# Sparse attention and a mixer on one core: VectorE with at most one SBUF operand, block sums and second remainders on GpSimd

## The chip, the cores and the metric

The kernel runs on one core of a Trainium2 chip. The core has a matrix engine (TensorE, PE in the profile), a vector engine (VectorE, DVE), an activation engine (ScalarE, ACT), a general engine (GpSimd, POOL) and a queue engine for transfers (SyncE, SP). PE reads SBUF and writes PSUM; DVE and ACT read and write both; POOL works on SBUF alone. The metric is the device time of one execution in microseconds. For the kernel before the change it is 271.68 us (median of three runs, 271.33 to 276.72).

## The reference

q, k and v have the shape 4 x 8 x 768 x 64 (batch, heads, positions, head size), in float32. Attention is sparse: the positions form 12 blocks of 64, and each query sees its own block and the three blocks with the highest gate.

```
k_rep  = k.reshape(B, H, 12, 64, D).mean(axis=3)
gate   = einsum(q, k_rep); blocks after the query's own get -1e9
sel    = the top 3 blocks of each query, and its own block
scores = q @ k.T / 8, only in selected blocks and at or before the query
x      = softmax(scores) @ v, heads side by side: (4, 768, 512)
u      = x + (relu(x^T @ w_tok1) @ w_tok2)^T
out    = u + relu(u @ w_ch1) @ w_ch2
```

A wrong choice of a block changes the output visibly, so the gate is computed to float32 accuracy.

## The kernel before

**Pairs.** The unit of attention is a pair of heads: 16 pairs, four to a batch. For each pair q and k are loaded (L473) and transposed on PE (`transposed`, L420, in float32; k of pairs 8 to 15 in half precision, L513). ACT or DVE evict the transposed q to QT (float32) and k to KA (L302 for ACT, L304 for DVE; both are lines of the helper `copy`). QT is cast to half precision into QA (`q16`, the group QA<-QT). The mask enters the scores as 12 more rows of the contraction: rows 64 to 75 of KA mark the block of a key, those of QA hold 0 for a block that is seen and -1 for others.

**Gate.** For pairs 0 to 7 the block sums of k come from a DVE reduction over the transposed k (L492). For pairs 8 to 15 `block_sums` loads the batch's keys once more (kb, L441) and halves them by additions (L449), copies the result (L453), transposes it (L454) and evicts it (L456). From pair 4 on (THIRDS) the gate is three bfloat16 products: q and the sums are split into a high part and two remainders (R1 at L555, R2 at L557 for q; `thirds_of`, L431 and L433, for the sums). PE forms them (L542 or L564), DVE adds the causal bias and the three parts (gm, L545 or L569), takes the eight largest of 12 (MAX8, L575, ten instructions a pair), compares with the third (ge, L577) and makes the 0 or -1 rows (bn, two instructions, L581). bn then goes to QA by PE transpositions and two evictions (L600, pairs 0 to 7) or by a DVE transpose and four small DMAs on SP (L586, L589, pairs 8 to 15, the set BDMA).

**Scores and mixers.** The scores (L621) go through the exponential on ACT (L628) into E, POOL clears what lies behind the diagonal (L636), PE multiplies with v (L645), and DVE divides (L648, L652). Token mixing is L663, L667, L677 and L680, the transposition of its result L688, L302 and L304. Channel mixing of a batch follows when its four pairs are done: L706 and L712 or L714, then L723 and L726, and the output leaves on SP (L729).

**PSUM.** Scores have two buffers of two banks. Everything else shares four banks (the ring R), of which channel mixing may hold three; at the end it gets the scores' banks too.

**Order.** The program is written out by a planner (`Plan`). Each step has a cost for each engine that may take it and a due time (`pr`): a pair's start, from EARLY and PACE, less a lead from the table L. The planner walks through time, gives each engine the due step that can start, and so fixes the engine of each step and the order on each engine. A step marked `port=True` is kept off the time of any GpSimd step by `shared`: the two take turns on the port. Where PE would be idle before channel mixing begins, filler matmuls on zeros are put in (L768). Steps run in this order on each engine, and waits between engines come from the data.

Of the kernel before, what the change touches and what calls it, by code (L numbers as in the profile page):

```python
# [9 lines left out]
FP = mybir.dt.float32  # L10
# [35 lines left out]
THIRDS = 4  # L46
BDMA = set(range(8, 16))
EARLY, PACE = 5.28, 14.41
L = dict(kd=28.39, qd=27.08, vd=11.34, va=-3.4, kt=12.9, kr=4.36, ke=-7.41, qt=14.51, qe=2.5, q16=14.89, g=13.38,
         b=7.0, k16=18.79, kx=22.66, kc=20.11, r=6.71, kb=28.92, ks=42.68, w1=-1.17, w2=0.38, wc1=18.04, wc2=24.91,  # L50
         tok=9.65, ml=13.72, o0=-3.85, o1=-3.08, o2=0.0, o3=4.03, o4=0.0, o5=2.8, o6=0.0, o7=0.0, o8=4.91, o9=0.0,
         o10=-8.96, o11=0.22, o12=-0.21, o13=-0.53, o14=-3.47, o15=0.77, m0=0.0, m1=0.47, m2=0.0, m3=3.31)
# [207 lines left out]
def kernel(  # L260
# [101 lines left out]
    ks2 = [sb([128, 2, NB], FP, f"ks2_{i}") for i in range(2)]  # L362
    ksr = Ring("ks2", ks2)
# [3 lines left out]
    kspr = Ring("ksp", [ksp])  # L367
    kppr = sring(2, [128, 3, 2, NB], BF, "kpp")
    ks3r = sring(2, [128, 3, NB], FP, "ks3")
# [3 lines left out]
    for t in ks2:  # L373
        nc.gpsimd.memset(t, 0.0)
# [11 lines left out]
    ks32r = sring(1, [128, 3, PPB * 2 * NB], FP, "ks32")  # L386
    ksar = sring(2, [128, NB], FP, "ksa")
    gmr = sring(2, [128, NJ - 1, 2 * NB], FP, "gm")
    m8r = sring(2, [128, NJ - 1, 2, 8], FP, "m8")
    ger = sring(2, [128, NJ - 1, 2 * NB], FP, "ge")  # L390
# [34 lines left out]
    def thirds_of(src, dst, part, rd, kp, pr):  # L425

        def split(e):
            t, o = src.t, ENG[e]
            h = t.bitcast(BF).rearrange("c i (n two) -> c i n two", two=2)[:, :, :, 1]
            for i in range(2):  # L430
                o.tensor_tensor(out=t[:, i + 1], in0=t[:, i], in1=h[:, i], op=ALU.subtract)  # L431
            for x in range(2):
                o.tensor_copy(out=dst(x), in_=part(h, x))  # L433
        P.op({"DVE": (760.0, 840.0), "POOL": (850.0, 930.0)}, split, port=True, rd=rd, wr=[(src, 2), (kp, 0), (kp, 1)], pr=pr)

    def block_sums(b, pr):

        kb, ksn, ks32, t, kp = Buf(kbr), Buf(ksnr), Buf(ks32r), Buf(Rr), Buf(kspr)
        P.op({"POOL": (80.0, 120.0)}, lambda: nc.gpsimd.memset(kb.t[0:1, 0:1], 0.0), wr=[(kb, 0)], pr=pr - L["kb"])
        P.op({"SP": (700.0, 1800.0, 96 * 1100.0 / 16)},  # L440
             lambda: nc.sync.dma_start(out=kb.t, in_=k[b].rearrange("h (n t) d -> (h n) (t d)", t=64)), wr=[(kb, 0)], pr=pr - L["kb"])  # L441
        n = 2048
        while n >= 64:
            step = min(n, 1024)
            for o in range(0, n, step):
                c = {"DVE": (step * 1.1 + 60, step * 1.1 + 140)}
                if n >= 512:
                    c["POOL"] = (step * 2.2 + 60, step * 2.2 + 140)
                P.op(c, lambda e, n=n, o=o, step=step: ENG[e].tensor_tensor(  # L449
                    out=kb.t[:, o:o + step] if n > 64 else ksn.t[:, 0, :], in0=kb.t[:, o:o + step], in1=kb.t[:, n + o:n + o + step], op=ALU.add),  # L450
                    port=True, rd=[(kb, 0)], wr=[(kb, 0)] if n > 64 else [(ksn, 0)], pr=pr - L["ks"])
            n //= 2
        P.op({"DVE": (190.0, 260.0)}, port=True, fn=lambda: nc.vector.tensor_copy(out=ksn.t[:, 1, :], in_=ksn.t[:, 0, :]), rd=[(ksn, 0)], wr=[(ksn, 9)], pr=pr - L["ks"])  # L453
        P.op(pe(slow=1), lambda: nc.tensor.transpose(out=t.t[:, 0:96], in_=ksn.t.rearrange("r g d -> r (g d)"), identity=id32[0:96, 0:96]),  # L454
             rd=[(ksn, 0), (ksn, 9)], wr=[(t, 0)], pr=pr - L["ks"] + 1)
        P.op(dve(96), lambda: nc.vector.tensor_copy(out=ks32.t[:, 0], in_=t.t[:, 0:96]),  # L456
             rd=[(t, 0)], wr=[(ks32, 0)], pr=pr - L["ks"] + 1)
        thirds_of(ks32, lambda x: kp.t[64 * x:64 * x + 64, :, :, x, :],
                  lambda h, x: h.rearrange("r i (q x n) -> r q i x n", q=PPB, x=2)[64 * x:64 * x + 64, :, :, x, :], [(ks32, 0)], kp, pr - L["ks"] + 1)
        return kp  # L460

    def pair(p):
# [4 lines left out]
        early, thirds = p < FIRST, p >= THIRDS  # L467
# [14 lines left out]
        if early:  # L482
            if thirds:
                ks3, kp = Buf(ks3r), Buf(kppr)
                ksa, sums = ks3, lambda i: ks3.t[:, 0, 6 * i:6 * i + 6]
            else:
                ksa, ks2b = Buf(ksar), Buf(ksr)
                sums = lambda i: ksa.t[:, 6 * i:6 * i + 6]
            for i in range(2):
# [3 lines left out]
                    out=sums(i), in_=t.t[:, 0:HS].rearrange("c (n w) -> c n w", w=64), axis=AX.X, op=ALU.add),  # L493
                    rd=[(t, 0)], wr=[(ksa, i)], pr=t0 - L["kr"])
# [4 lines left out]
            if thirds:  # L499
                thirds_of(ks3, lambda x: kp.t[64 * x:64 * x + 64, :, x, :], lambda h, x: h[64 * x:64 * x + 64], [(ks3, 0), (ks3, 1)], kp, t0 - L["kr"] + 0.1)  # L500
            else:
                for x in range(2):
                    P.op({"DVE": (170.0, 220.0)}, port=True, fn=lambda x=x: nc.vector.tensor_copy(out=ks2b.t[64 * x:64 * x + 64, x, :], in_=ksa.t[64 * x:64 * x + 64, :]),
                         rd=[(ksa, 0), (ksa, 1)], wr=[(ks2b, x)], pr=t0 - L["kr"] + 0.1)
# [15 lines left out]

        for i in range(2):
# [15 lines left out]
        gm, m8, ge, bn = Buf(gmr), Buf(m8r), Buf(ger), Buf(bnr)  # L537
# [9 lines left out]
        else:  # L547
            R1, R2 = Buf(R1r), Buf(R2r)
# [3 lines left out]

            def high(t):
                return t.bitcast(BF).rearrange("c (n two) -> c n two", two=2)[:, :, 1]
            P.op({"DVE": (760.0, 840.0), "POOL": (1210.0, 1290.0)}, port=True, fn=lambda e: ENG[e].tensor_tensor(out=R1.t, in0=QT.t[:, 128:S], in1=high(QT.t[:, 128:S]), op=ALU.subtract),  # L555
                 rd=[(QT, 0), (QT, 1)], wr=[(R1, 0)], pr=t0 - L["r"])
            P.op({"DVE": (760.0, 840.0), "POOL": (1210.0, 1290.0)}, port=True, fn=lambda e: ENG[e].tensor_tensor(out=R2.t, in0=R1.t, in1=high(R1.t), op=ALU.subtract),  # L557
                 rd=[(R1, 0)], wr=[(R2, 0)], pr=t0 - L["r"] + 0.1)

            def gate():  # L560
                for j in range(NJ - 1):
                    s = slice(128 * j, 128 * j + 128)
                    for i, a in enumerate([high(QT.t[:, 128:S])[:, s], high(R1.t)[:, s], R2.t[:, s]]):
                        nc.tensor.matmul(out=g.t[:, 3 * W2 * j:3 * W2 * j + 3 * W2], lhsT=a,  # L564
                                         rhs=kpt().rearrange("c i x n -> c (i x n)"), start=(i == 0), stop=(i == 2))
            P.op(pe(*[72] * 15), gate, rd=[(QT, 0), (QT, 1), (R1, 0), (R2, 0), (kp, 0), (kp, 1)], wr=[(g, 0)], pr=t0 - L["g"])
# [4 lines left out]

        def top():
            for j in range(NJ - 1):
                for x in range(2):
                    nc.vector.max(out=m8.t[:, j, x, :], in_=gm.t[:, j, NB * x:NB * x + NB])  # L575
        P.op({"DVE": (730.0, 820.0)}, top, rd=[(gm, 0)], wr=[(m8, 0)], pr=t0 - L["g"] + 0.2)
        P.op({"DVE": (220.0, 300.0)}, port=True, fn=lambda: nc.vector.tensor_tensor(  # L577
            out=ge.t.rearrange("p j (x n) -> p j x n", n=NB), in0=gm.t.rearrange("p j (x n) -> p j x n", n=NB),
            in1=m8.t[:, :, :, 2:3].broadcast_to([128, NJ - 1, 2, NB]), op=ALU.is_ge), rd=[(gm, 0), (m8, 0)], wr=[(ge, 0)], pr=t0 - L["g"] + 0.3)
        for x in range(2):  # L580
            P.op({"DVE": (180.0, 240.0)}, port=True, fn=lambda x=x: nc.vector.scalar_tensor_tensor(  # L581
                out=bn.t[:, 1:, x, 0:NB], in0=ge.t[:, :, NB * x:NB * x + NB], scalar=1.0,
                in1=own[:, :, NB * x:NB * x + NB], op0=ALU.subtract, op1=ALU.max), rd=[(ge, 0), (fixed, "cst")], wr=[(bn, x)], pr=t0 - L["g"] + 0.4)
        if p in BDMA:
            bnt = Buf(bntr)
            P.op({"DVE": (520.0, 600.0)}, lambda: nc.vector.transpose(  # L586
                out=bnt.t.rearrange("p j x n -> p (j x n)"), in_=bn.t.rearrange("p j x n -> p (j x n)")), rd=[(bn, 0), (bn, 1)], wr=[(bnt, 0)], pr=t0 - L["b"])
# [6 lines left out]
        else:  # L594
# [6 lines left out]
            P.op(pe(*[128] * 5), btr, rd=[(bn, 0), (bn, 1)], wr=[(bt, 0)], pr=t0 - L["b"])  # L601
# [210 lines left out]
```

## Time and profile before

| | before |
|---|---|
| median of the runs | 271.68 us |
| the profiled execution | 271.58 us |
| its span, first to last instruction | 269.9 us |
| PE busy | 254.8 us (94%) |
| DVE busy | 180.6 us (67%) |
| ACT busy | 161.0 us (60%) |
| POOL busy | 116.1 us (43%) |
| granted clock | 0.999 |

A row of a group names a line, an engine, an operation and tiles (output<-input), then its count, busy time, the mean of one in ns, and the idle time of the engine ahead of it with what ended it. Ends of matmuls are modelled, so PE's busy time overlaps a little. 1.7 us of the execution's time lie outside the span.

### The profile page before, as it was taken

How to read it: one execution, taken by the hardware profiler on the slowest of the kernel's cores; microseconds unless marked ns; L12 is line 12 of the kernel's file. 1: busy time of each engine (PE TensorE's matmuls, PEld its weight loads, DVE VectorE, ACT ScalarE, POOL GpSimd, SP SyncE). 2: the span in 40 equal slices, each digit the busy share in tenths (PEclk: the TensorE clock that was granted, in tenths of full speed). 3: DMA queues.
4: the chain of work that ended last, by engine and by line, in shares of the span. 5: the costliest groups of instructions: out<-in, count | busy, mean ns of one | idle time of the engine just before them, and what ended most of it. 6: DMA issues, size and time to landing. Idle time of an engine off the chain costs nothing.

```text
span 269.9 us, 6806 instructions
## 1 busy us (share of the span) xinstructions
PE 254.8 (94%) x2634; PEld 174.9 (65%) x2634; DVE 180.6 (67%) x545; ACT 161.0 (60%) x259; POOL 116.1 (43%) x194
## 2 busy tenths in 40 slices
PE   7799999989999998979999899999999999999993
PEld 7677877766676665736777466767666665554541
DVE  5899999997697688897788565859657532301102
ACT  2679989846674684448983467466675471260520
POOL 7137866885364855573685343445152020000000
PEclk9999999999999999999999999999999999999999
DMA  8999989979907999514999740111001200212103
GB/s 169 222 216 197 234 187 227 233 186 192 188 3 198 217 230 238 123 39 116 178 175 221 177 115 5 41 44 41 5 4 43 83 2 0 78 41 78 39 0 118
DMA packets 87088, 33.10 MB, mean 123 GB/s; under 512 B 80592, under 2 KB 83280, under 8 KB 86864
## 3 DMA queue, kind: packets, MB, share of 16 engines
q1 hardware_dynamic: 82112, 28.22, 47.6%
q0 software_dynamic: 3232, 3.93, 8.5%
q10 hardware_dynamic: 1712, 0.52, 1.0%
q8 instruction: 20, 0.33, 0.5%
q14 instruction: 12, 0.10, 0.1%
HBM read 30.01 MB, written 6.29 MB: 135 GB/s over the span
## 4 chain that ended last, share of the span: by engine, by line
PE 74%; DVE 13%; ACT 5%; issue 3%; DMA 3%; SPq 1%; POOL 1%; DVEq 0%
PE pm L706 17%; PE pm L723 14%; PE sc L621 11%; PE pm L645 6%; PE sc L723 5%; PE pm L420 4%; ACT E L628 3%; PE pm L677 3%; PE pm L663 3%; PE sc L706 3%; PE pm L564 2%; DVE bn L581 2%; DMA k<-in_k_dram 2%; DVE QA L304 2%; DVE u L680 2%
## 5 line engine op out<-in xcount | busy, mean ns | idle before, releaser
L628 ACT ACTIVATE E<-sc 128x1024 f16<-128x1024 f32 (+1 forms) x96 | 84.0, 920 | 16.2 <-PE sc L621 15.2
L636 POOL TENSOR_SCALAR_AFFINE_SELECT E<-E 128x256 f16<-128x256 f16 x96 | 41.1, 435 | 73.5 <-ACT E L628 72.7
L706 PE MATMUL pm<-uT,wc 128*128 128x384 f16 x340 | 64.8, 326 | 1.9 <-DVE os L726 1.9
L723 PE MATMUL pm<-wc,h 128*128 128x512 f16 x228 | 59.5, 379 | 0.0
L706 PEld LDWEIGHTS <-wc 128*128 128x128 f16 x384 | 36.3, 98 | 26.1 <-issue 2.6
L621 PE MATMUL sc<-QA,KA 76*128 76x512 f16 (+3 forms) x256 | 49.2, 305 | 1.5 <-DMA QA<-bnt 1.1
L712 ACT ACTIVATE h<-pm 128x384 f16<-128x384 f32 x60 | 29.6, 493 | 24.0 <-PE pm L706 23.8
L723 PEld LDWEIGHTS <-h 128*128 128x128 f16 x288 | 26.8, 98 | 23.0 <-issue 1.0
L621 PEld LDWEIGHTS <-KA 76*128 76x128 f16 x256 | 22.9, 98 | 16.5 <-DMA QA<-bnt 1.5
L645 PEld LDWEIGHTS <-E 128*128 128x128 f16 x672 | 24.9, 98 | 3.9 <-POOL ks L431 0.8
L645 PE MATMUL pm<-VA,E 128*128 128x65 f16 x651 | 25.6, 193 | 0.5 <-POOL ks L431 0.5
L304 DVE CAST QA<-QT 64x768 f16<-64x768 f32 x22 | 17.9, 812 | 5.9 <-ACT QT L302 5.5
L726 DVE TENSOR_TENSOR os<-u,sc 128x512 f32<-128x512 f16 x5 | 3.3, 687 | 26.0 <-PE sc L723 26.0
L726 DVE TENSOR_TENSOR os<-u,pm 128x512 f32<-128x512 f16 x19 | 12.9, 681 | 11.1 <-PE pm L723 9.6
L714 DVE TENSOR_SCALAR h<-pm 128x384 f16<-128x384 f32 x25 | 13.7, 554 | 8.5 <-PE pm L706 8.0
L479 POOL CAST VA<-v 128x768 f16<-128x768 f32 x16 | 13.3, 837 | 12.6 <-DMA v<-in_v_dram 9.3
L652 DVE TENSOR_TENSOR x<-pm,rc 128x384 f16<-128x384 f32 x31 | 17.2, 554 | 0.8
L302 ACT COPY QT<-pm 128x384 f32<-128x384 f32 x26 | 11.9, 484 | 9.0 <-PE pm L420 8.3
L680 DVE TENSOR_TENSOR u<-x,pm 128x384 f16<-128x384 f16 x30 | 15.5, 548 | 2.5 <-PE pm L677 2.4
L723 PE MATMUL sc<-wc,h 128*128 128x512 f16 x60 | 15.1, 379 | 0.3 <-DVE x L652 0.3
L420 PE MATMUL pm<-id,q 128*128 128x128 f32 x96 | 14.5, 275 | 0.0
L557 POOL TENSOR_TENSOR R<-R 128x640 bf16<-128x640 f32 x10 | 13.4, 1344 | 1.9 <-DVE R L555 1.6
(93 smaller groups left out, 369.2 us busy)
## 6 DMA issues: line engine op xcount, KB each, us to landing
k<-in_k_dram SPq DMA_DIRECT2D x32, 192.0 KB
v<-in_v_dram SPq DMA_DIRECT2D x16, 384.0 KB
out_dram<-os SPq DMA_DIRECT2D x24, 256.0 KB
q<-in_q_dram SPq DMA_DIRECT2D x30, 192.0 KB
wc<-in_moe_w_ch_dram POOLq DMA_DIRECT2D x8, 384.0 KB, 7.5
kb<-in_k_dram SPq DMA_DIRECT2D x2, 1536.0 KB
w<-in_moe_w_tok_dram POOLq DMA_DIRECT2D x2, 384.0 KB, 7.2
QA<-bnt SPq DMA_DIRECT2D x32, 9.0 KB
```

Of the source, the lines that this page charges most:

```text
L304: e.tensor_copy(out=out, in_=in_)
L420: nc.tensor.transpose(out=t[:, 128 * j:128 * j + 128], in_=src.t[:, 3 * i + j].rearrange("p x d -> p (x d)"), identity=id32)
L621: nc.tensor.matmul(out=s.t[:, at:at + 128 * m], lhsT=KA.t[:, x, 128 * kk:128 * kk + 128], rhs=QA.t[:, q0:q0 + m, x, :], start=True, stop=True)
L628: nc.scalar.activation(out=E.t[:, 1024 * g_:1024 * g_ + WIDTH[g_]], in_=s.t[:, 0:WIDTH[g_]], func=AF.Exp, scale=scale)
L636: nc.gpsimd.affine_select(out=o, in_=o, pattern=[[0, 2], [1, 128]], compare_op=ALU.is_ge, fill=0.0, base=0, channel_multiplier=-1)
L645: nc.tensor.matmul(out=t[:, jq, :], lhsT=E.t[:, cc:cc + 128], rhs=VA.t[:, x, kk, :], start=(kk == 0), stop=(kk == jq))
L652: P.op(dve(384), lambda a=a, rc=rc, x=x: nc.vector.tensor_tensor(out=xp.t[:, :, 64 * x:64 * x + 64], in0=a.t[:, 0:NJ * 65].rearrange("p (j ...
L680: P.op(dve(128 * n), lambda m=m, j0=j0, n=n: nc.vector.tensor_tensor(out=u.t[:, c, j0:j0 + n, :], in0=xp.t[:, j0:j0 + n, :], in1=m.t[:, 0: ...
L706: nc.tensor.matmul(out=m.t[:, 0:HS], lhsT=wc1[:, c, 128 * f:128 * f + 128], rhs=uT.t[:, c, HS * i:HS * i + HS], start=(c == 0), stop=(c == ...
L712: nc.scalar.activation(out=h2.t[:, f, :], in_=m.t[:, 0:HS], func=AF.Relu)
L723: nc.tensor.matmul(out=m.t, lhsT=h2.t[:, f, 128 * jj:128 * jj + 128], rhs=wc2[:, f, :], start=(f == 0), stop=(f == NFC - 1))
L726: P.op(dve(DM), lambda j=j, m=m, o=o: nc.vector.tensor_tensor(out=o.t.rearrange("p (c d) -> p c d", d=128), in0=u.t[:, :, j, :], in1=m.t.r ...
```

## The change

The comparison writes 0 or 1 for "below the third largest" into the gate's PSUM bank, MAX8 writes there too, and the bias step is one product of that with `own`. The remainder R1 is taken from the transposed q in PSUM, half by half; R2 is GpSimd's alone. The reduction of pairs 0 to 3 writes to PSUM, and a product with a mask of ones (`side`) replaces the two copies. Block sums in steps of at most 512 columns, their copy and the splits are GpSimd's. The casts of q may go to ACT too. Pairs 4 to 7 use the DMA path for bn. The leads and start offsets in L have other values, and with them the planner's order is another one throughout: the kernel has 67 filler matmuls in place of 100, DVE takes 11 casts of q in place of 22, GpSimd 6 in place of 10 and ACT 15 in place of none.

```diff
-THIRDS = 4
-BDMA = set(range(8, 16))
-EARLY, PACE = 5.28, 14.41
+EARLY, PACE = 5.1, 13.21
...
+         m3=1.67, th=4, bd=4)
...
+    side = sb([128, 2, 6], FP, "side")
+    nc.gpsimd.memset(side, 0.0)
+    for x in range(2):
+        nc.gpsimd.memset(side[64 * x:64 * x + 64, x], 1.0)
...
-        P.op({"DVE": (760.0, 840.0), "POOL": (850.0, 930.0)}, split, port=True, rd=rd, wr=[(src, 2), (kp, 0), (kp, 1)], pr=pr)
+        P.op({"POOL": (850.0, 930.0)}, steps, rd=rd, wr=[(src, 2), (kp, 0), (kp, 1)], pr=pr)
...
-            step = min(n, 1024)
+            step = min(n, 512)
             for o in range(0, n, step):
-                c = {"DVE": (step * 1.1 + 60, step * 1.1 + 140)}
-                if n >= 512:
-                    c["POOL"] = (step * 2.2 + 60, step * 2.2 + 140)
-                P.op(c, lambda e, n=n, o=o, step=step: ENG[e].tensor_tensor(
+                P.op({"POOL": (step * 2.15 + 60, step * 2.15 + 140)}, lambda n=n, o=o, step=step: nc.gpsimd.tensor_tensor(
...
+                if not thirds:
+                    P.op({"DVE": (150.0, 220.0)}, lambda t=t, i=i: nc.vector.tensor_tensor(
+                        out=ks2b.t[:, :, 6 * i:6 * i + 6], in0=t.t[:, HS:HS + 6].rearrange("c (o n) -> c o n", o=1).broadcast_to([128, 2, 6]),
+                        in1=side, op=ALU.mult), rd=[(t, 1)], wr=[(ks2b, i)], pr=t0 - L["kr"] + 0.1)
...
+            if thirds:
+                a, z = (128, HS) if i == 0 else (HS, S)
+                P.op(dve(z - a), lambda t=t, i=i, a=a, z=z: nc.vector.tensor_tensor(
+                    out=R1.t[:, a - 128:z - 128], in0=t.t[:, a - HS * i:z - HS * i], in1=upper(QT.t[:, a:z]), op=ALU.subtract),
+                    rd=[(t, 0), (QT, i)], wr=[(R1, i)], pr=t0 - L["r"])
...
-            P.op({"POOL": (800.0, 860.0), "DVE": (500.0, 580.0)}, q16, port=True, rd=[(QT, 0), (QT, 1)], wr=[(QA, (x, 0))], pr=t0 - L["q16"])
+            P.op({"POOL": (800.0, 860.0), "DVE": (500.0, 580.0), "ACT": (680.0, 780.0)}, q16, port=True, rd=[(QT, 0), (QT, 1)], wr=[(QA, (x, 0))], pr=t0 - L["q16"])
...
+            P.op({"POOL": (1210.0, 1290.0)}, lambda: nc.gpsimd.tensor_tensor(out=R2.t, in0=R1.t, in1=upper(R1.t), op=ALU.subtract),
+                 rd=[(R1, 0), (R1, 1)], wr=[(R2, 0)], pr=t0 - L["r"] + 0.1)
...
+        m8 = lambda: g.t[:, 384:464].rearrange("p (j x n) -> p j x n", x=2, n=8)
+        below = lambda: g.t[:, 0:W2 * (NJ - 1)].rearrange("p (j x n) -> p j x n", x=2, n=NB)
...
-        P.op({"DVE": (220.0, 300.0)}, port=True, fn=lambda: nc.vector.tensor_tensor(
-            out=ge.t.rearrange("p j (x n) -> p j x n", n=NB), in0=gm.t.rearrange("p j (x n) -> p j x n", n=NB),
-            in1=m8.t[:, :, :, 2:3].broadcast_to([128, NJ - 1, 2, NB]), op=ALU.is_ge), rd=[(gm, 0), (m8, 0)], wr=[(ge, 0)], pr=t0 - L["g"] + 0.3)
-        for x in range(2):
-            P.op({"DVE": (180.0, 240.0)}, port=True, fn=lambda x=x: nc.vector.scalar_tensor_tensor(
-                out=bn.t[:, 1:, x, 0:NB], in0=ge.t[:, :, NB * x:NB * x + NB], scalar=1.0,
-                in1=own[:, :, NB * x:NB * x + NB], op0=ALU.subtract, op1=ALU.max), rd=[(ge, 0), (fixed, "cst")], wr=[(bn, x)], pr=t0 - L["g"] + 0.4)
-        if p in BDMA:
+        P.op({"DVE": (220.0, 300.0)}, lambda: nc.vector.tensor_tensor(
+            out=below(), in0=gm.t.rearrange("p j (x n) -> p j x n", n=NB), in1=m8()[:, :, :, 2:3].broadcast_to([128, NJ - 1, 2, NB]), op=ALU.is_lt),
+            rd=[(gm, 0), (g, 1)], wr=[(g, 0)], pr=t0 - L["g"] + 0.3)
+        P.op({"DVE": (220.0, 300.0)}, lambda: nc.vector.tensor_tensor(
+            out=bn.t[:, 1:, :, 0:NB], in0=below(), in1=own.rearrange("p j (x n) -> p j x n", n=NB), op=ALU.mult),
+            rd=[(g, 0), (fixed, "cst")], wr=[(bn, 0)], pr=t0 - L["g"] + 0.4)
+        if p >= L["bd"]:
```

More of the change, by code (lines that the diff above doesn't have):

```diff
@@ L423, in halves, with upper, split, steps @@
         return slice(HS * i, HS * i + HS)
-    def thirds_of(src, dst, part, rd, kp, pr):
-        def split(e):
-            t, o = src.t, ENG[e]
+    def upper(t):
+        return t.bitcast(BF).rearrange("c (n two) -> c n two", two=2)[:, :, 1]
+    def split(src, dst, part, rd, kp, pr):
+        def steps():
+            t, h = src.t, [upper(src.t[:, i]) for i in range(3)]
+            for i in range(2):
+                nc.gpsimd.tensor_tensor(out=t[:, i + 1], in0=t[:, i], in1=h[i], op=ALU.subtract)
             h = t.bitcast(BF).rearrange("c i (n two) -> c i n two", two=2)[:, :, :, 1]
-            for i in range(2):
-                o.tensor_tensor(out=t[:, i + 1], in0=t[:, i], in1=h[:, i], op=ALU.subtract)
             for x in range(2):
-                o.tensor_copy(out=dst(x), in_=part(h, x))
-        P.op({"DVE": (760.0, 840.0), "POOL": (850.0, 930.0)}, split, port=True, rd=rd, wr=[(src, 2), (kp, 0), (kp, 1)], pr=pr)
+                nc.gpsimd.tensor_copy(out=dst(x), in_=part(h, x))
+        P.op({"POOL": (850.0, 930.0)}, steps, rd=rd, wr=[(src, 2), (kp, 0), (kp, 1)], pr=pr)
     def block_sums(b, pr):
@@ L466, in pair @@
         t0 = T(p) + L[f"o{p}"]
-        early, thirds = p < FIRST, p >= THIRDS
+        early, thirds = p < FIRST, p >= L["th"]
         q32, k32, v32 = Buf(q32r), Buf(k32r), Buf(v32r)
@@ L482, in pair @@
         if early:
[L483 to L488, printed above, removed]
+            ks2b = kp = Buf(kppr if thirds else ksr)
+            ks3 = Buf(ks3r) if thirds else None
             for i in range(2):
@@ L499, in pair @@
             if thirds:
-                thirds_of(ks3, lambda x: kp.t[64 * x:64 * x + 64, :, x, :], lambda h, x: h[64 * x:64 * x + 64], [(ks3, 0), (ks3, 1)], kp, t0 - L["kr"] + 0.1)
-            else:
-                for x in range(2):
-                    P.op({"DVE": (170.0, 220.0)}, port=True, fn=lambda x=x: nc.vector.tensor_copy(out=ks2b.t[64 * x:64 * x + 64, x, :], in_=ksa.t[64 * x:64 * x + 64, :]),
-                         rd=[(ksa, 0), (ksa, 1)], wr=[(ks2b, x)], pr=t0 - L["kr"] + 0.1)
+                split(ks3, lambda x: kp.t[64 * x:64 * x + 64, :, x, :], lambda h, x: h[64 * x:64 * x + 64], [(ks3, 0), (ks3, 1)], kp, t0 - L["kr"] + 0.1)
         else:
```

55 lines of the change are left out of this document (21 added, 34 removed).

## The prediction

> **What bounds the kernel now.** I read the slices of the page first, to see which engine is full in which stage.
>
> ```profile
> PE   7799999989999998979999899999999999999993
> ...
> DVE  5899999997697688897788565859657532301102
> ...
> DMA  8999989979907999514999740111001200212103
> ```
>
> PE is full nearly everywhere, VectorE (DVE) and the DMA engines only in the first eight or nine slices of 6.75 us. I cut the span at the first real transposition (6.24 us), at the first channel matmul (L706, 56.96 us) and where the last matmuls are issued (264.16 us). The view by windows gives busy time (and count) of PE, PE's weight loads, DVE, ACT and POOL, then clock, DMA share and GB/s:
>
> ```profile
> 6.24:56.96 50.72, 47.33 (x648) 39.56 (x649) 47.86 (x166) 41.35 (x63) 31.28 (x60) 1.00 1.11 209
> 56.96:264.16 207.20, 201.41 (x1938) 130.32 (x1936) 128.50 (x370) 118.15 (x194) 79.91 (x115) 1.00 0.44 100
> ```
>
> The first of these stretches (call it early) is paced by DVE: 47.86 of 50.72 us busy, with ACT at 41.35, and PE padded with filler matmuls on zeros. The second (late) belongs to PE: 201.41 of 207.20 us, so 5.79 us idle is all that a faster DVE or GpSimd (POOL) can return there. The clock is full (1.00), so it is no term. The chain of waits names most of those 5.79 us (total us, times, longest); PE's rows:
>
> ```profile
> PE pm L706 <- DVE os L726: 1.9, 1, 1.9
> ...
> PE sc L621 <- DMA QA<-bnt: 1.1, 1, 1.1
> ...
> PE pm L564 <- DVE ksp L433: 0.9, 1, 0.9
> ...
> PE pm L600 <- DVE bn L581: 0.8, 1, 0.8
> ```
>
> The largest, 1.9 us, shows what the change is about. The timelines of DVE, POOL and PE there (start, length, instruction):
>
> ```profile
> 116.64 3.48 DVE L581 SCALAR_TENSOR_TENSOR bn<-ge,cst 128x60 f16<-128x60 f32 x2
> ```
>
> ```profile
> 114.40 1.81 POOL L555 TENSOR_TENSOR R<-QT 128x640 f32<-128x640 f32 x1 [1.68 <-ACT QT L302]
> 116.29 1.45 POOL L557 TENSOR_TENSOR R<-R 128x640 bf16<-128x640 f32 x1
> 117.70 2.34 POOL L449 TENSOR_TENSOR kb<-kb 96x1024 f32<-96x1024 f32 x1
> ```
>
> ```profile
> 120.76 0.81 PE L706 MATMUL pm<-uT,wc 128*128 128x384 f16 x4 [1.93 <-DVE os L726]
> ```
>
> Two tiny bias steps last 3.48 us and end (120.12) just as POOL's 2.34 us addition ends (120.04). The eviction queued behind them (os) is late, and PE stands. By tile (min/median/max ns) this is a pattern:
>
> ```profile
> L581 DVE SCALAR_TENSOR_TENSOR bn<-ge,cst x32: 206/218/2378, 14.0 to 207.6; 128x60 f16<-128x60 f32 x32
> L304 DVE CAST QA<-QT x22: 533/554/1517, 9.4 to 200.2; 64x768 f16<-64x768 f32 x22
> L577 DVE TENSOR_TENSOR ge<-gm,m x16: 270/280/579, 13.4 to 206.9; 128x120 f32<-128x120 f32 x16
> L569 DVE TENSOR_TENSOR gm<-pm,cst x12: 276/283/283, 39.4 to 205.1; 128x120 f32<-128x120 f32 x12
> ```
>
> DVE instructions with both operands in SBUF, or copying SBUF to SBUF, stretch to 2 to 11 times their median; those with one operand in PSUM (gm) never do: 276 to 283 ns.
>
> **The change part by part.** Prices are from these groups by form (count, busy us, mean ns):
>
> ```profile
> L636 POOL TENSOR_SCALAR_AFFINE_SELECT E<-E 128x256 f16<-128x256 f16 x96 | 41.1, 435 | 73.5 <-ACT E L628 72.7
> ...
> L304 DVE CAST QA<-QT 64x768 f16<-64x768 f32 x22 | 17.9, 812 | 5.9 <-ACT QT L302 5.5
> L652 DVE TENSOR_TENSOR x<-pm,rc 128x384 f16<-128x384 f32 x31 | 17.2, 554 | 0.8
> ...
> L557 POOL TENSOR_TENSOR R<-R 128x640 bf16<-128x640 f32 x10 | 13.4, 1344 | 1.9 <-DVE R L555 1.6
> ...
> L479 POOL CAST VA<-v 128x768 f16<-128x768 f32 x16 | 13.3, 837 | 12.6 <-DMA v<-in_v_dram 9.3 <-PE pm L645 2.7 <-PE pm L663 0.5
> ...
> L575 DVE MAX8 m<-gm 128x8 f32<-128x12 f32 x160 | 13.2, 158 | 0.3
> ...
> L581 DVE SCALAR_TENSOR_TENSOR bn<-ge,cst 128x60 f16<-128x60 f32 x32 | 10.6, 368 | 0.2
> ...
> L302 ACT COPY KA<-pm 64x768 f16<-64x768 f16 x10 | 7.9, 794 | 1.6 <-PE pm L513 1.5
> ...
> L449 POOL TENSOR_TENSOR kb<-kb 96x1024 f32<-96x1024 f32 x3 | 7.0, 2344 | 0.0
> ...
> L586 DVE STREAM_TRANSPOSE bnt<-bn 128x384 f16<-128x384 f16 x8 | 4.6, 573 | 0.1
> ...
> L449 DVE TENSOR_TENSOR kb<-kb 96x1024 f32<-96x1024 f32 x3 | 4.3, 1420 | 0.0
> ...
> L555 DVE TENSOR_TENSOR R<-QT 128x640 f32<-128x640 f32 x5 | 4.2, 848 | 0.0
> ...
> L600 PE MATMUL pm<-id,bn 128*64 128x128 f16 x40 | 3.7, 224 | 0.8 <-DVE bn L581 0.8
> ...
> L668 DVE TENSOR_SCALAR h<-pm 128x256 f16<-128x256 f32 x4 | 1.7, 418 | 0.8 <-PE pm L663 0.8
> ...
> L449 POOL TENSOR_TENSOR kb<-kb 96x512 f32<-96x512 f32 x1 | 1.3, 1267 | 0.0
> ...
> L431 POOL TENSOR_TENSOR ks<-ks 128x96 f32<-128x96 f32 x2 | 0.7, 348 | 0.1
> ```
>
> *Costs the trace does not show.* The comparison and the bias step now read PSUM: nearest are 0.283 (gm) and 0.418 (128x256), taken 0.283, since the size is gm's. The bias step's two halves (10.6/32 = 0.33 each) become one, so a pair saves 0.66 - 0.28 = 0.38 us of DVE. MAX8 into PSUM: 0.083 each as now (13.2/160), or 0.158 if PSUM writes do not overlap, 0.075 x 10 = 0.75 us a pair; taken 0.083, as it reads the same data; 0 to 12 us of DVE over 16 pairs stays in the range. The remainder R1 becomes 0.418 + 0.554 = 0.97 us on DVE in place of 0.85 there or a GpSimd step. The 64x768 cast of q that ACT may now take: 0.794 from PSUM, and 0.418 to 1.0 as outer ends; taken 0.794.
>
> The Trainium skill ("VectorE: DVE Perf Modes", section on the TRN2 errata) speaks against moving operands: it gives VectorE 58 cycles plus length from SBUF but 120 from PSUM, by estimate 62/0.96 = 65 ns more for each of 64 instructions (24 R1, 16 comparisons, 16 bias steps, 8 block masks), 4.1 us of DVE in all. This trace disagrees: 280 ns (ge, both in SBUF) against 283 (gm, one in PSUM), 0.2 us in all.
>
> *Early stretch.* The program's own order of instructions (read from the built program, engine by engine) holds in the changed kernel, up to the first channel matmul, the same 30 exponentials and 30 masks, but one pair's gating more. ACT gets six casts of q, 6 x 0.794 = +4.8 us (its other differences cancel): 41.35 + 4.8 = 46.1 of 50.72. DVE: two casts less -1.1; bias steps 10 x 0.33 against 6 x 0.28, -1.6; one maximum, comparison and final addition more, 0.83 + 0.28 + 0.28 = +1.4; two transposes +1.1; six R1 pieces against two whole steps 2.9 - 1.7 = +1.2; one split of four small steps less, -1.1 at 0.28; eight block masks for eight copies, at most +0.9; three q evictions more, one reduction less (+1.1 at 0.554) and four smaller evictions less (-1.7 at 0.418). Sum about +0.2. Casts blocked by GpSimd cost 0.812 on the mean against a median of 0.554, so the five of this stretch lose up to 1.3 us that may go. DVE thus stays at 46.8 to 48.1, ACT rises to 46.1: from one pacing engine to two. GpSimd keeps its 31 of 50.72 (two casts of q less, one R2 more). I take 0.5 us won, bounds -2.9 (all DVE idle, 50.72 - 47.86, squeezed out) to +4.8 (every added ACT cast lands on the path).
>
> *Late stretch.* Distances on PE are counted in matmuls between two places of the program's order, each group at its spacing in the chain, as the channel groups with 0.65 us:
>
> ```profile
> 64.31 0.65 PE pm L706 x4
> ```
>
> Pairs 4 to 7 also leave PE's bias transposition: 20 of 40 matmuls, 3.7/2 = 1.85 us, three quarters of it here: 1.4. The idle waits: 1.9 goes (the bias steps have PSUM operands, and the second remainder and sums beside them block nothing); 0.8 goes (the transposition waited for belongs to pair 5, which takes the DMA path); 1.1 goes, because the order puts pair 11's gate 18.9 us of matmuls ahead of its scores, against 12.5 now. Together 3.8, leaving 5.79 - 3.8 = 2.0.
>
> What comes: the block sums, on GpSimd alone. For batch 2 they are seven additions of 512, 7 x 1.267 = 8.9, and by the slope between 512 and 1024 (2.1 ns a column, 0.19 fixed) 0.73 + 0.46 + 0.33 for the short ones, a copy by the same 0.3: 10.7 us. Between the first of them and the split the order sets six masks 2.6, one R2 1.3, three casts 2.5, the split itself 1.4 (4 x 0.35): 18.5 us of GpSimd. PE has 17.7 us of matmuls from there to pair 8's gate (L564), plus some 0.5 for the transposition and its copy. So that gate is about 1.3 us late with no mask waiting; this takes the place of the 0.9 that stood there. Batch 3's sums end 12 us of matmuls ahead of their gate and cost nothing. For waits that a new order brings elsewhere I allow half of what is left, 1.0. Late idle: 2.0 - 0.9 + 1.3 + 1.0 = 3.4 in place of 5.79. DVE itself has room here (128.50 of 207.20 us), so the R1 pieces it gains and the sums it loses cost and bring nothing beyond the waits named.
>
> *SP's queue.* Pairs 4 to 7 add 16 small DMAs, four in a row. The queue's own timeline, and a landing in the chain:
>
> ```profile
> 163.18 3.31 SPq L589 DMA_DIRECT2D QA<-bnt  x4
> ```
>
> ```profile
> 48.44 8.13 SPq L441 DMA_DIRECT2D kb<-in_k_dram  x1
> ```
>
> ```profile
> 152.83 2.00 DMA QA<-bnt
> ```
>
> Each group holds SP 3.3 us, and until it is ready the loads of q and v behind it wait, in a stretch where DMA share is above 1 and one load needed 8.13 us to issue. It is covered as long as gate and scores of these pairs stand apart: 12.6, 15.5, 13.2 and 10.4 us of matmuls in the changed order (7.3, 5.4, 7.8, 7.7 now), against some 3 us of DVE, 3.3 of issue and 2 of landing. Without that cover each pair costs up to 5 us.
>
> *PSUM banks.* The gate's bank is now held through maximum, comparison and bias step, 0.83 + 0.28 + 0.28 = 1.4 us longer a pair, and q's two banks until the R1 pieces are done, up to 0.97. Transpositions, gates, attention outputs and the mixers share four banks, so PE may stand for a free one. No row of before names such a wait. Late, channel matmuls on other banks keep PE fed; early I bound it by 0 and four pairs at 1.4, 5.6 us, and take nothing, because the early order also puts gates of pairs 4 and 5 some 5 to 10 us further ahead of their scores than before. That end, 272.9, lies within the range.
>
> *Sum.* 56.96 - 0.5 = 56.5; late 201.41 - 1.4 + 3.4 = 203.4; tail as before, 269.9 - 264.16 = 5.74: a span of 265.6 us. The profiled execution took 271.58 us with a span of 269.9, so 1.7 lies outside, and it is 0.1 below the median 271.68. Predicted: 267.3 us.
>
> **The rivals.**
>
> *The full gain.* Late idle nearly vanishes (below 0.5) and early DVE loses all its idle: 54.1 + 200.5 + 5.74 + 1.7 = 262. For: every named wait involves a blocked DVE. Against: DMA and ACT are close behind.
>
> *ACT takes over early.* Half of the added casts land on the path, +2.4: 59.4 + 203.4 + 5.74 + 1.7 = 270.2. For: ACT reaches 91% of the stretch. Against: 9.4 us idle now.
>
> *The blocking stays.* If GpSimd also held instructions with one SBUF operand, the 3.8 would stay: 271.1. Against: gm never stretches.
>
> *Slower: GpSimd becomes the bound at batch 2's sums.*
>
> ```profile
> POOL E L636 <- ACT E L628: 72.7, 57, 7.8
> ```
>
> Its masks are queued between the additions and it waits for exponentials: 72.7/57 = 1.3 us a time now. If all six waits fall into that chain, the gate is 1.3 + 7.6 = 8.9 us late: 267.3 + 7.6 = 274.9. It decides from 4.4 us beyond my 1.3. For: no spare time in that chain. Against: when PE stands, its exponentials are long done, so waits shrink. The Trainium skill ("GPSIMD Engine Reference", section on engine selection) advises VectorE for two-input elementwise work, GpSimd being about twice as slow; the trace agrees less strongly, 2344 against 1420 ns for 1024 columns.
>
> **How the numbers follow.** Forecast (265 to 269.5) 0.45, full gain (261.5 to 265) 0.22, ACT or blocking (269.5 to 272.5) 0.20, slower (up to 279) 0.13. Two per cent, about what a measurement of this kernel can tell from no change, is 266.2 below and 277.1 above. Faster beyond it: the full gain and a quarter of the forecast, 0.34; slower beyond it: the upper part of the last case, 0.09; within: 0.57. The range leaves out the far halves of the outer cases: 262.5 to 273.5.
>
> **What would show it.** Right: the bias step at one length near 0.28 us; no PE wait for os; late PE idle near 3.4 us; PE waiting for ksp about 1 us; first channel matmul near 56.5 us. Wrong: ACT near 95% before it and its start beyond 58 us; MAX8 groups above 1.2 us; PE waiting for ksp or QA<-bnt several us; stretched DVE steps with a PSUM operand.

## The result, and the profile after

The changed kernel takes 284.04 us (median of four runs, 282.82 to 285.27) where the kernel before took 271.59 beside it (271.33 to 276.72): a ratio of 1.046, 95% interval 1.039 to 1.053. One execution of the kernel before, the one of 276.72 us, ran in a slower state and is not in the ratio. The changed kernel is slower, and the 267.3 us predicted lie far off. The profiled execution took 282.82 us with a span of 281.1.

The same two stretches in the view by windows, cut at the first real transposition (6.31 us), the first channel matmul (68.06) and the issue of the last matmuls (275.40); columns as before:

```profile
6.31:68.06 61.75, 51.98 (x616) 42.19 (x617) 51.90 (x171) 45.67 (x69) 29.95 (x63) 0.89 0.90 157
68.06:275.40 207.34, 199.29 (x1915) 128.87 (x1913) 115.06 (x335) 120.60 (x195) 79.79 (x137) 1.00 0.48 105
```

The early stretch is 11.0 us longer (61.75 against 50.72). The late one is as long as before, though PE has 2.1 us less to do: its idle time is 8.05 us where 3.4 was forecast. The clock is 0.89 in the first. The page's busy times, its slices and its chain of waits, by line:

```profile
PE 257.8 (92%) x2581; PEld 176.3 (63%) x2581; DVE 171.7 (61%) x516; ACT 167.8 (60%) x265; POOL 115.1 (41%) x216
...
PE   7579798989998999888999999899898999999994
...
DVE  5785799999777563898575676837758351301002
...
PEclk9996689999999999999999999999999999999998
```

```profile
PE pm L702 16%; PE pm L719 13%; PE sc L617 10%; DVE pm L572 9%; PE sc L719 5%; PE pm L641 5%; PE pm L418 5%; DMA k<-in_k_dram 3%; PE sc L702 3%; DVE gm L563 3%; PE pm L673 3%; PE pm L659 2%; DVE x L648 2%; PE pm L684 2%; PE pm L542 1%
```

L572 is MAX8, and its 9% are by far the largest entry of any engine but PE. Its group, then one pair's ten in the timeline, in the changed kernel:

```profile
L572 DVE MAX8 pm<-gm 128x8 f32<-128x12 f32 x160 | 29.1, 182 | 5.3
```

```profile
10.85 2.13 DVE L572 MAX8 pm<-gm 128x8 f32<-128x12 f32 x10
```

and the same ten in the kernel before:

```profile
12.31 0.82 DVE L575 MAX8 m<-gm 128x8 f32<-128x12 f32 x10
```

Ten take 2.13 us in place of 0.82. From one start to the next, (0.82 - 0.157) / 9 = 0.074 us became (2.13 - 0.18) / 9 = 0.216, which is longer than the instruction itself (0.182). That is 1.31 us a pair, 20.9 us of VectorE over 16 pairs. PE's waits in the late stretch of the changed kernel (total us, times, longest), all of 0.8 us or more:

```profile
PE pm L702 <- DVE bn L577: 1.2, 1, 1.2
PE pm L507 <- DVE R L525: 1.1, 1, 1.1
PE pm L702 <- DVE x L648: 1.1, 1, 1.1
PE pm L673 <- DVE x L648: 0.9, 1, 0.9
PE pm L719 <- DVE bn L577: 0.9, 1, 0.9
PE pm L673 <- DVE os L722: 0.8, 1, 0.8
PE pm L641 <- DVE bn L577: 0.8, 1, 0.8
```

The first of them in the timelines of DVE and PE:

```profile
129.68 2.13 DVE L572 MAX8 pm<-gm 128x8 f32<-128x12 f32 x10
131.85 0.29 DVE L574 TENSOR_TENSOR pm<-gm,pm 128x120 f32<-128x120 f32 x1
132.17 0.28 DVE L577 TENSOR_TENSOR bn<-pm,cst 128x120 f16<-128x120 f32 x1
```

```profile
132.50 1.46 PE L702 MATMUL pm<-uT,wc 128*128 128x384 f16 x8 [1.21 <-DVE bn L577]
```

A channel matmul does not read bn. It waits for the gate's bank, which it is to write and which the bias step is the last to read: the maxima delay that step by 1.3 us, and PE waits 1.21.

Of PE's four longest pauses in the early stretch three lie behind maxima too. Two of them are shown here, the first with the ACT step that it goes back to. VectorE's maxima ran from 10.85 to 12.98 us, and its reductions (L486) behind them until 13.90. The next maxima ran from 17.47 to 19.60, ahead of a block mask (L490):

```profile
14.31 0.52 PE L418 MATMUL pm<-id,q 128*128 128x128 f32 x3 [2.21 <-ACT QT L301]
```

```profile
13.47 0.47 ACT L301 CAST KA<-pm 64x384 f16<-64x384 f32 x1 [1.67 <-DVE pm L486]
```

```profile
20.37 0.90 PE L418 MATMUL pm<-id,k 128*128 128x128 f32 x3 [1.21 <-DVE ks L490]
```

Why the ten became slow is seen in the built program, not in the profile. This is what each instruction on VectorE waits for, before the change and after it:

```
before   Max m8<-gm 128x8       [waits DVE]
         Max m8<-gm 128x8  x9
after    Max pm<-gm 128x8  x10  [waits DVE]
```

With the maxima in SBUF the first waits for gm, and nine follow freely. With the maxima in PSUM each one waits for VectorE's own semaphore (the counter by which an engine tells that an instruction has ended), that is for the end of the one before it. The program orders the ten writes to one bank, though they go to different columns; ten writes to different columns of one SBUF tile it leaves free.

### The profile page after: what moved, and what is told of

The parts are those of the page before. It is cut to its first block, busy times and chain, and to the rows that moved or that the text cites. A ratio compares the mean times of both kernels' runs of the same rounds, so it can differ in the third digit from the quotient of the medians.

```text
span 281.1 us, 6723 instructions
## 1 busy us (share of the span) xinstructions
PE 257.8 (92%) x2581; PEld 176.3 (63%) x2581; DVE 171.7 (61%) x516; ACT 167.8 (60%) x265; POOL 115.1 (41%) x216
## 4 chain that ended last, share of the span: by engine, by line
PE 68%; DVE 21%; issue 4%; DMA 3%; ACT 1%; POOL 1%; SPq 0%; DVEq 0%
PE pm L702 16%; PE pm L719 13%; PE sc L617 10%; DVE pm L572 9%; PE sc L719 5%; PE pm L641 5%; PE pm L418 5%; DMA k<-in_k_dram 3%; PE sc L702 3%; DVE gm L563 3%; PE pm L673 3%; PE pm L659 2%; DVE x L648 2%; PE pm L684 2%; PE pm L542 1%
## 5 line engine op out<-in xcount | busy, mean ns | idle before, releaser
L632 POOL TENSOR_SCALAR_AFFINE_SELECT E<-E 128x256 f16<-128x256 f16 x96 | 38.6, 409 | 80.4 <-ACT E L624 80.0
L702 PE MATMUL pm<-uT,wc 128*128 128x384 f16 x332 | 62.3, 326 | 2.4 <-DVE bn L577 1.2
L719 PE MATMUL pm<-wc,h 128*128 128x512 f16 x216 | 56.3, 379 | 1.2 <-DVE bn L577 0.9
L708 ACT ACTIVATE h<-pm 128x384 f16<-128x384 f32 x64 | 31.4, 491 | 23.5 <-PE pm L702 22.1
L572 DVE MAX8 pm<-gm 128x8 f32<-128x12 f32 x160 | 29.1, 182 | 5.3
L448 POOL TENSOR_TENSOR kb<-kb 96x512 f32<-96x512 f32 (+2 forms) x18 | 19.9, 1115 | 1.0 <-DMA kb<-in_k_dram 1.0
L551 POOL TENSOR_TENSOR R<-R 128x640 bf16<-128x640 f32 x12 | 15.0, 1252 | 10.9 <-DVE R L525 10.7
L525 DVE TENSOR_TENSOR R<-pm,QT 128x256 f32<-128x256 f32 (+1 forms) x24 | 11.3, 486 | 10.6 <-ACT QT L301 10.5
L673 PE MATMUL pm<-h,w 128*128 128x128 f16 x186 | 14.2, 219 | 3.5 <-DVE h L664 1.0
L719 PE MATMUL sc<-wc,h 128*128 128x512 f16 x72 | 16.6, 379 | 0.0
```

The lines of the kernel that those rows point to most:

```text
L448: P.op({"POOL": (step * 2.15 + 60, step * 2.15 + 140)}, lambda n=n, o=o, step=step: nc.gpsimd.tensor_tensor(out=kb.t[:, o:o + step] if n > ...
L572: nc.vector.max(out=m8()[:, j, x, :], in_=gm.t[:, j, NB * x:NB * x + NB])
L632: nc.gpsimd.affine_select(out=o, in_=o, pattern=[[0, 2], [1, 128]], compare_op=ALU.is_ge, fill=0.0, base=0, channel_multiplier=-1)
L673: nc.tensor.matmul(out=m.t[:, 128 * j:128 * j + 128], lhsT=w2[:, t, 128 * (j0 + j):128 * (j0 + j) + 128], rhs=h1.t[:, t, :], start=(t == 0 ...
L702: nc.tensor.matmul(out=m.t[:, 0:HS], lhsT=wc1[:, c, 128 * f:128 * f + 128], rhs=uT.t[:, c, HS * i:HS * i + HS], start=(c == 0), stop=(c == ...
L708: nc.scalar.activation(out=h2.t[:, f, :], in_=m.t[:, 0:HS], func=AF.Relu)
```

## The experiments

In the three groups of runs the kernel before itself took anything from 270.2 to 280.7 us, so the kernels below are compared with one another, and only the last paragraph of this section compares with it.

**The thresholds back in SBUF**, with every engine's order left as in the changed kernel:

```diff
+    m8s = [sb([128, NJ - 1, 2, 8], FP, f"m8_{i}") for i in range(2)]
-        m8 = lambda: g.t[:, 384:464].rearrange("p (j x n) -> p j x n", x=2, n=8)
+        m8 = lambda: m8s[p % 2]
```

> The changed kernel with one edit: the ten MAX8 of a pair write their thresholds into an SBUF tile, as before the change; the comparison reads them there. The order of every engine is that of the changed kernel. Theory A (a MAX8 into PSUM starts 0.216 us after the last one in place of 0.075, and these 1.3 us a pair hold up the gates of the early pairs, so that TensorE idles and its clock is lowered): a group of ten takes about 0.8 us again, the first channel matmul comes near 57 us in place of 68.06, the granted clock stays above 0.95 early, and the time is 268 to 274 us. Theory B (the loss lies in the other edits and in the new order: the casts of q on ScalarE, the block sums and second remainders on GpSimd, the other leads): the groups take 0.8 us too, but the first channel matmul stays beyond 65 us and the time above 280 us.

Measured: 267.6 us (265.97 to 269.56). The group, the two stretches, and all of PE's listed waits in the late one:

```profile
L573 DVE MAX8 m<-gm 128x8 f32<-128x12 f32 x160 | 13.1, 157 | 0.3
```

```profile
6.20:59.12 52.92, 47.95 (x616) 39.37 (x617) 46.69 (x171) 45.44 (x69) 29.82 (x63) 0.97 1.06 183
59.12:258.94 199.82, 198.42 (x1916) 129.28 (x1914) 106.53 (x335) 120.11 (x195) 80.19 (x137) 1.00 0.50 109
```

```profile
PE pm L642 <- POOL E L633: 1.1, 2, 0.7
```

The whole loss hangs on where the maxima go, with every other edit in place. The early stretch is 8.8 us shorter than in the changed kernel, the late one 7.5; the waits for bn, R and x are gone. Theory B falls. The first channel matmul came at 59.12, not quite at the 57 expected, and the clock did not stay up throughout: its mean early is 0.97, but it was at half from about 27 to 30.5 us.

**The same change in the kernel before**, and its twin with the bank kept as long but the maxima in SBUF (the last line; in both kernels the planner lays out the steps anew, and the two orders are the same):

```diff
-        gm, m8, ge, bn = Buf(gmr), Buf(m8r), Buf(ger), Buf(bnr)
+        gm, ge, bn = Buf(gmr), Buf(ger), Buf(bnr)
+        m8 = lambda: g.t[:, 384:464].rearrange("p (j x n) -> p j x n", x=2, n=8)
...
+        m8 = lambda: m8s[p % 2]
```

> The kernel before with one edit: the ten MAX8 of a pair write into columns 384 to 463 of the bank that holds the pair's gate, and the comparison reads them there; the bank is kept until then, and the planner lays the steps out anew with that. Theory A: a group of ten takes about 2.1 us in place of 0.8, and the time is 6 to 16 us above that of its twin, in which the bank is kept as long but the thresholds are in SBUF, with a lower granted clock early. Theory B: within 2 us of the twin.

> The twin: the kernel before, with the bank of a pair's gate kept until the comparison is done, as if the thresholds were in it, but with the thresholds in SBUF; the planner's order is that of the run with the thresholds in PSUM. It tells what the longer hold of the bank and the new order cost by themselves. Theory A: within 3 us of the kernel before (268 to 275 us). Theory A2 (banks held longer are what costs): 277 us or more.

Measured: 289.43 us (288.74 to 291.65) with the maxima in PSUM, 274.22 (273.73 to 275.56) for the twin. The one edit costs 15.2 us in a kernel that has none of the other edits, as theory A had it (6 to 16). Its ten MAX8 take 2.13 us, the twin's 0.82. Keeping the bank until the comparison, and the new order, cost far less: the twin takes 3.5 us more than the fastest execution of the kernel before in this group (270.70; the others took 277.4 to 278.9).

**VectorE's time without PSUM.** Seventeen more MAX8 into SBUF behind each ten, which nobody reads:

```diff
+            for i in range(17):
+                nc.vector.max(out=m8w[:, i % 10, :], in_=gm.t[:, i % 5, 0:NB])
```

> The kernel with the thresholds in SBUF, and behind each pair's ten MAX8 seventeen more that write an SBUF tile which nobody reads: 17 x 0.075 = 1.3 us of VectorE a pair, the time that the writes to PSUM cost, without a write to PSUM. Theory A, by VectorE's time alone: the time is back at 281 to 287 us, with the first channel matmul near 68 us and the granted clock low after 20 us. Theory A2 (a write to PSUM does its harm by holding a bank or a port that others need, not by VectorE's time): within 3 us of the kernel with the thresholds in SBUF.

Measured: 284.26 us (282.83 to 284.94), first channel matmul at 69.92. The padding in the timeline:

```profile
11.53 1.31 DVE L576 MAX8 m8w<-gm 128x8 f32<-128x12 f32 x17
```

The clock was 0.50 from 20 to 30 us. So 1.31 us a pair on VectorE, without any maxima in PSUM, is worth the whole loss: theory A, not A2.

**The wait without PSUM.** The maxima stay in SBUF, but each overlaps the last one, so that the program makes each wait (its listing shows ten waits again):

```diff
-                    nc.vector.max(out=m8()[:, j, x, :], ...
+                    nc.vector.max(out=m8s[p % 2][:, 10 * j + 5 * x:10 * j + 5 * x + 8], ...
```

> The kernel with the thresholds in SBUF, with one more edit: each MAX8 writes its eight values five columns behind the last one's, over the last three of them, so that every one of the ten has to wait for the end of the one before it, as the ten in the changed kernel do (there each waits because the program orders all writes to one PSUM bank; with the thresholds in SBUF only the first of ten waits). No write goes to PSUM, and the third largest, the only one that is read, is as before. Theory C (the wait of each MAX8 for the last, not the memory that it writes to, is the 0.14 us): a group of ten takes 1.9 to 2.2 us, 0.2 from start to start, and the time is 279 to 287 us. Theory D (the write to PSUM itself keeps the next MAX8 from starting): a group takes 0.8 us and the time stays within 2 us of 267.6.

Measured: 284.49 us (283.52 to 285.28). Ten of them:

```profile
11.32 2.06 DVE L573 MAX8 m<-gm 128x8 f32<-128x12 f32 x10
```

Theory C holds: the wait alone makes 0.82 us into 2.06, and the remaining 0.07 is all that is left for the memory. The opposite trial, writes to one PSUM bank without the waits, was not made. That a write to PSUM need not hold up the next instruction is seen in the reductions of the early pairs, whose two writes go to two banks and wait for no VectorE instruction: two into PSUM (555 ns each) take 1.01 us in the changed kernel, and two into SBUF (550 ns) 1.02 in the kernel before:

```profile
12.89 1.01 DVE L486 TENSOR_REDUCE pm<-pm 128x6 f32<-128x384 f32 x2
```

```profile
43.18 1.02 DVE L492 TENSOR_REDUCE ks<-pm 128x6 f32<-128x384 f32 x2
```

The Trainium skill ("VectorE: DVE Perf Modes", section "The DRAIN you can't avoid") says that the next VectorE instruction doesn't start before the last one's pipeline is empty, but that one which isn't held back starts earlier, and that a semaphore between two costs nothing extra, from eight copies with and without it. The rows here agree with the earlier start (0.074 us from start to start, for an instruction of 0.157) and not with the free semaphore: 0.82 us for ten MAX8 without the wait, 2.06 with it.

**The clock.** Two tries put matmuls of zeros ahead of the four early steps that PE waited longest for, in the changed kernel: first in the banks that the transpositions use, then in those of the scores. The diff is that of the second.

```diff
+MORE = {("g", 0, 0): 16, ("q", 1, 1): 30, ("k", 3, 1): 18, ("g", 3, 0): 20}
...
+        n = max(n, more.get(o.n, 0))
+        if more.get(o.n):
+            junk = sc[min((0, 1), key=lambda i: Sr.avail[i])][:, 0:120]
```

> The changed kernel, thresholds in PSUM, with matmuls of zeros (16, 34, 22 and 26) put ahead of the four early steps before which TensorE idled 1.2 to 2.2 us; nothing else moves. Theory A with the clock as an amplifier: the granted clock stays above 0.9 from 20 to 40 us, where it was 0.67, some 13 us at half clock go, which are worth up to 6.5 us of matmuls, and the time is 275 to 281 us, still 8 us or more above the kernel with the thresholds in SBUF, since VectorE's own delay stays. Theory E (the clock is the whole early loss): below 274 us. Theory F (the clock costs nothing, since VectorE sets the pace): within 2 us of 284.

> The changed kernel, thresholds in PSUM, again with matmuls of zeros (16, 30, 18, 20) ahead of the four early steps that TensorE waited longest for, but now in the banks of the scores: in the last try they stood in banks that VectorE reads, and one of its steps waited 1.2 us for them. If the clock is an amplifier of the delay (theory A), the clock stays above 0.95 to 40 us and the time falls to 276 to 281 us. If VectorE's chain sets the pace whatever TensorE's clock is (theory F), the time stays within 2 us of 284 with the clock up.

Measured: 285.75 us (283.55 to 288.35) for the first and 281.62 (279.88 to 283.12) for the second. In the first the clock was up (0.99 or more from 10 to 40 us) and nothing was won: its first channel matmul came at 68.78 us, so by its own expectation theory F held. But it brought a harm of its own. One of VectorE's early waits in that run:

```profile
DVE ks L493 <- PE pm L770: 1.2, 1, 1.2
```

L770 are the zeros, in a bank that VectorE was to read. The second has no such wait; its stretches:

```profile
6.13:65.16 59.03, 51.87 (x705) 43.16 (x705) 51.99 (x171) 45.72 (x69) 30.05 (x63) 1.00 0.94 165
65.16:272.90 207.74, 199.69 (x1917) 129.10 (x1915) 115.49 (x335) 120.59 (x195) 79.95 (x137) 1.00 0.49 105
```

At full clock the first channel matmul comes at 65.16 in place of 68.06, 2.9 us earlier, and the late stretch doesn't move. So of the 16.8 us between the spans of the changed kernel and of its version with SBUF maxima (281.1 and 264.3), the lowered clock holds some 2.9 and VectorE's waits some 13.9: 6.0 early (65.16 - 59.12), 7.9 late. These are single executions; the medians give the clock 2.4 us, and the version with SBUF maxima had lost a little of its own clock. Theory A's 276 to 281 was a little low, theory F's 2 us a little narrow.

The reverse, no zeros after the first 7 us in the kernel with SBUF maxima (`b > 7000.0` added to the conditions on which `fill` returns nothing; 18 matmuls go):

> The kernel with the thresholds in SBUF, without the 20 matmuls of zeros behind the first 7 us that the plan lays into TensorE's early gaps; VectorE's work is not touched. Theory A with the clock as an amplifier: TensorE idles longer, the granted clock falls to half for some 5 to 15 us early, and the time rises by 2 to 7 us to 270 to 275 us. Theory F: the clock may fall, but the time stays within 1 us of 267.6.

Measured: 271.55 us (270.23 to 272.92), clock 0.55, 0.50 and 0.59 in the three windows from 10 to 40 us, first channel matmul at 66.76. In this kernel a clock at about half for most of 30 us costs 4 us.

**The true price in the plan**, 2.05 us in place of 0.73:

```diff
-        P.op({"DVE": (730.0, 820.0)}, top, ...
+        P.op({"DVE": (2050.0, 2140.0)}, top, ...
```

> The changed kernel with one number changed: the planner is told that the ten MAX8 of a pair take 2.05 us in place of 0.73, so that it lays out all steps and fills TensorE's gaps with the true price. Theory A: the planner can fill the gaps and take work ahead, but VectorE has 21 us more work and is 0.94 busy early; the time falls by 3 to 8 us, to 276 to 281 us, not to 268. Theory G (an order laid out for a wrong price is the whole loss): below 271 us.

Measured: 284.31 us (280.82 to 287.12). Two executions took 280.82 and 283.32, the other two 285.29 and 287.12, so the expected gain of 3 to 8 us is not shown, and theory G falls. The first channel matmul was earlier in the profiled execution (65.60), the fastest of the four, but the late stretch was no shorter (207.90 us).

**What the rest of the change is worth**, from the kernel with SBUF maxima: the comparison's result in SBUF too (an SBUF pair `bls` in place of `below`'s view of the bank); the sums of batches 2 and 3 shared out between VectorE and GpSimd again (the old cost table `c` back in `block_sums`, with a new order from the planner); and zeros ahead of three early steps (`MORE` with 16, 12 and 10).

> The kernel with the thresholds in SBUF, with the result of the comparison there too: comparison and bias step take two SBUF operands each, the order is unchanged. If an operand in PSUM is worth nothing beside the prices seen (comparison 283 ns before and 280 after), the time is within 1.5 us of 267.6. If keeping VectorE off the port that it shares with GpSimd is what won the 4 us, both steps grow where GpSimd is at work, and the time is 269 to 272 us.

> The kernel with the thresholds in SBUF, with the block sums of batches 2 and 3 shared out between VectorE and GpSimd as before the change; the planner lays out the steps anew. If moving the sums to GpSimd is what won the time of the late stage, its idle time of TensorE is back at 4 us or more and the time is 269 to 273 us; if the other edits did (the new order with no transposition of the bias by TensorE, the subtraction from PSUM), it is within 1.5 us of 267.6.

> The kernel with the thresholds in SBUF, with matmuls of zeros (16, 12 and 10) ahead of three early steps that TensorE waited 0.6 to 1.2 us for; they go to the banks of the scores, which VectorE does not use. Its clock was lowered from 27 to 30.5 us in the profiled run and for longer in the runs that took 269 us. If the clock is what parts these, the granted clock stays at 0.99 or above in all runs and the median falls by 1 to 3 us, to 264.5 to 266.5; if not, it stays at 267 to 269.

Measured: 266.03 us (265.24 to 267.39), 269.65 (267.09 to 272.65) and 268.87 (266.06 to 269.59). With two SBUF operands the bias step and, beside it, the one with one:

```profile
L579 DVE TENSOR_TENSOR bn<-bl,cst x16: 271/284/877, 12.7 to 197.3; 128x120 f16<-128x120 f32 x16
```

```profile
L578 DVE TENSOR_TENSOR bn<-pm,cst x16: 262/279/283, 13.0 to 198.1; 128x120 f16<-128x120 f32 x16
```

One stretch to 877 ns returns and costs nothing in the end. With the sums shared the median is 2.0 us higher, but the ranges overlap, and PE's late idle time is 2.33 us (200.98 less 198.65), not the 4 or more that was expected if the sums had won the late stage; so it isn't shown that moving them to GpSimd won it. The zeros won nothing: two of six executions kept the clock at 1.00 and took 266.1 and 267.2 us, four had 0.979 to 0.985 and took 268.5 to 269.6. What sets it off there stays open.

The kernel with no thresholds in PSUM at all (266.03 us) has the lowest median of all: its slowest run (267.39) lies below every run of the kernel before, and the ratio to the runs of the kernel before in the same group is 0.960, 95% interval 0.955 to 0.965. In that group the kernel before took 275.43 to 280.46 us; against the 271.59 of the first group the gain would be 2.0%.

## Why the prediction was wrong, point by point

**MAX8 into PSUM: the term that failed.** I took "0.083, as it reads the same data", nothing added, with 0.75 us a pair as the outer bound. It measured 1.31 a pair, beyond the bound. Nor did the bound stand anywhere in the sum, though VectorE had only 50.72 - 47.86 = 2.86 us of idle time early and six gates to serve there. I had asked whether writes to PSUM overlap, a question about the memory; what came was a wait that the program adds, and whose cost is the instruction's whole length (0.182) plus a gap of some 0.034, not a rest of 0.158. I had read the built program for the order of its instructions, and not for what each one waits for, where it stands.

**The clock as "no term".** It was full before. In the changed kernel it fell while PE stood for a VectorE step behind the maxima (the 1.21 us until 20.37, after 2.21 until 14.31), and with zeros in those gaps it stayed up. It cost some 2.9 us, by the run with zeros in the scores' banks. That a late VectorE also slows PE was no part of the sum.

**PSUM banks, taken at nothing.** Right by itself late (there the kernel with SBUF maxima shows no wait for a bank held by the gate), wrong with the slow maxima: the three waits of 0.8 us or more for bn in the late stretch (1.2, 0.9, 0.8) are waits for that bank, since none of the matmuls reads bn. So "DVE itself has room here" did not protect PE: VectorE was busy 115.06 of 207.34 us, and PE waited for it all the same.

**The late stretch without that term.** The version with SBUF maxima shows what the sum would have met: 199.82 us with 1.40 idle, where I had 203.4 with 3.4. The waits that I had let go did go. The late gate of pair 8, 1.3 us by GpSimd's sums, did not come: none of PE's listed waits there is for the sums. PE's own work fell by 3.0, not 1.4.

**The early stretch.** 59.12 in place of 56.5, with SBUF maxima. ScalarE's 46.1 came close (45.44), and the rival in which it takes over did not come; VectorE had 46.69, not 46.8 to 48.1. So 267.6 us beside the predicted 267.3 is partly luck: 2.6 too little early, 3.6 too much late.

**Blocking.** Steps with one SBUF operand never stretched (262/279/283), as forecast. But that they gain by it was argued, not shown, and for the comparison and the bias step it isn't so: with two SBUF operands the kernel is as fast. This does not price the old blocking, since GpSimd's additions are now steps of 1.27 us in place of 2.34; and R1 and the block masks were not tried. The 3.8 us of waits went with the change without its maxima in PSUM; how much by which part of it is not settled.

**The rivals.** GpSimd's sums as the bound, the full gain and staying blocks: none of them came. The slower side had a chance of 0.09, and a mechanism that was not this one. The 1420 ns that I set against GpSimd's 2344 is a mean of 1834, 1216 and 1209; against the last two GpSimd takes 1.9 times as long. Of my signs, one had named the cause: "MAX8 groups above 1.2 us" (2.13). Another came by half: the first channel matmul "beyond 58 us" (68.06), but with ScalarE busy 74% before it, not 95%.

## What to carry to other kernels

When an edit moves where an instruction writes, look in the built program at what each instruction now waits for: a run of short ones loses its overlap if each must see the end of the last, and here ten lost 1.3 us together. Then ask what is queued behind such a run and who waits for that: 20.9 us more of VectorE cost some 14 us, the clock aside, although VectorE was busy only 61% of the span. The matrix engine that waited for it lost clock as well, so a stretch that was at full clock before is no proof that the clock is no term.

## What was not expected of the hardware

A wait of a VectorE instruction for the one directly before it costs 0.135 us for MAX8 on 12 columns (from start to start 0.209 against 0.074 us, both in SBUF). Into PSUM, with the wait, it is 0.216: the memory makes 7 ns.

The clock fell to half without any long pause of PE. In the changed kernel, by windows of 1 us (PE busy, its matmuls, clock, DMA share, GB/s):

```profile
12.00:13.00 1.00, 0.10 (x1) 1.00 1.35 217
13.00:14.00 1.00, 0.00 (x0) 1.00 1.35 218
...
18.00:19.00 1.00, 0.53 (x5) 1.00 1.34 224
19.00:20.00 1.00, 0.16 (x2) 0.92 1.10 177
20.00:21.00 1.00, 0.63 (x3) 0.50 0.93 206
```

The longest pause ahead of this fall was 2.21 us, and the clock was back at 1.00 by 27 us. It fell again at 30 us, in a pause of 1.35, and was back by 37. The kernel with SBUF maxima lost its clock at 27 us (0.53 in that window) with no pause above 0.64 us in the ten before. The Trainium skill ("TensorE: Matmul & The Clock Gate", Part 1) has the clock go to half after an idle window of about 3.4 us. The half agrees (0.50); the pause doesn't. What the clock answers to is not read off PE's pauses alone here, and stays open.
